# Element-strided squares and wider final stores in a fused attention and feed-forward kernel

## The chip, the cores and the metric

The kernel runs on one core of a Trainium2 chip. The metric is the device time of one execution in microseconds (us), the median over runs. Three runs of the kernel before gave 187.44, 187.94 and 187.97 us, so the median is 187.94 us.

A core has five engines that run side by side and wait for each other by semaphores. TensorE (PE in the profile; its weight loads are shown apart as PEld) multiplies matrices. ScalarE (ACT) and VectorE (DVE) compute elementwise. GpSimd (POOL) does small copies and memsets here. SyncE (SP) issues DMAs; ACT can issue DMAs too, on a hardware queue of its own.

## The reference, cut to what matters

```
phi(x)  = outer product of (S1 x) and (S2 x)          # 8 x 8 = 64 features per token
num     = phi(q) (phi(k)^T v),  den = phi(q) sum(phi(k)) + 1e-6
x       = num / den, heads side by side               # 4352 tokens x 128
h       = max(x @ w_in, 0)                            # 4352 x 2048
out     = (h * h) @ w_out                             # 4352 x 128, float32
```

The batch has 4 sequences of 1088 tokens. The part that matters here is the last line: each hidden value is rectified, squared, and multiplied by `w_out`.

## The kernel before, in words

Attention fills `xT`, which holds x transposed: 128 features on the partitions, 4352 token columns. Column 32·i + t of a sequence (t below 32, i below G = 34) is token 34·t + i, so 32 neighbouring columns are tokens that stand 34 apart in DRAM.

The feed-forward part walks over these columns in ten chunks (`FC`, line 135). Most are 448 or 512 columns wide; the first and the last are 256. The hidden width 2048 is cut into NB = 16 blocks of 128. A **unit** (line 560) is a chunk with as many blocks as fit into 512 result columns. The last chunk has 8 units of two blocks, called u0 to u7 here. A unit goes through four steps:

1. `ffn1` (L582): two matmuls, `w_in` block times the chunk's columns, into a PSUM tile `pg`. There are two such tiles in turn, so a unit's `ffn1` waits until the `relu` two units earlier has emptied its tile.
2. `relu` (L591), always on ACT: `pg` to the SBUF tile `gt`.
3. `square` (L599 on ACT or L601 on DVE): `gt` to the SBUF tile `g2`, which the profile names `g`. Its 512 columns are written in order.
4. `ffn2` (L615 in the last chunk, L620 in the others): accumulates over all 16 blocks. In the last chunk `g2` is the stationary operand, so that the result `po` comes out with tokens on the partitions: two token tiles of 128, the first in `po`, the second in `pol`.

A planner, `_Order.run` (lines 25 to 101), fixes the order of the instructions on each engine from estimated costs and due times. It decides which squares go to ACT and which to DVE. TensorE's own order is written out (lines 1043 to 1052): the two blocks of unit u in `ffn2` alternate with the two blocks of unit u + 4 in `ffn1` (LU = 4). For the last two units, all their blocks of the first token tile come before those of the second (line 1044), so the first tile is complete some 0.9 us earlier.

`f_last` (L642) then ends the kernel. ACT copies the first tile from PSUM to `obl` (L658), and `store(0)` sends it out; DVE copies the second tile (L660), and `store(1)` sends that. Column 32·x + t of a tile is on partition 32·x + t, so `store` (L648) issues four DMAs of 32 partitions, each going to 32 tokens that stand 34 rows apart: two on the SP queue and two on the ACT queue. A row is 128 floats, 512 bytes. The program ends when SP has seen the last DMA land (L1079).

Of the kernel before, what the change touches and what calls it, by code (L numbers as in the profile page):

```python
# [14 lines left out]
def _ap(t: bass.AP, p0: int, np_: int, off: int, free):  # L15
    p = list(t.ap)[0]
    return bass.AP(
        t.tensor, t.offset + p0 * p[0] + off, [[p[0], np_]] + [list(d) for d in free]
    )
# [85 lines left out]
def kernel(  # L105
# [11 lines left out]
    nc = tc.nc  # L117

    B, H, S, D = 4, 4, 1088, 32
    G = S // 32  # L120
# [20 lines left out]
    mult = mybir.AluOpType.mult  # L141
# [4 lines left out]
    Square = mybir.ActivationFunctionType.Square  # L146
# [111 lines left out]
    for i in range(2):  # L258
# [6 lines left out]
        out=own_f[:, :], in_=_ap(iden, 0, 128, 0, [[8, 16], [1, 8]]), op=add, axis=AX  # L265
# [13 lines left out]
    def banks(t_, x, col, n, k=2):  # L279

        return _ap(t_, 0, 128, 512 * x + col, [[512, k], [1, n]])
# [278 lines left out]
    units, first_unit, dur = [], {}, []  # L560
# [13 lines left out]
    last = len(FC) - 1  # L574
# [19 lines left out]
    def square(u, eng):  # L594
        w = units[u][2] * units[u][4]
        g2 = fpool.tile([128, 512], F32, tag="g2", bufs=G2, name="g2")
        gt = st["gt", u]
        if eng == "ACT":
            nc.scalar.activation(g2[:, 0:w], gt[:, 0:w], Square)  # L599
        else:  # L600
            nc.vector.tensor_tensor(out=g2[:, 0:w], in0=gt[:, 0:w], in1=gt[:, 0:w], op=mult)  # L601
        g2s[u] = g2

    def ffn2(u, i, xs=None):
# [37 lines left out]
    def f_last(c0):  # L642
        po, b = st["po", c0], B - 1


        def store(i):
            for x, eng in enumerate((nc.sync, nc.scalar, nc.sync, nc.scalar)):
                eng.dma_start(  # L648
                    bass.AP(
                        out.tensor,  # L650
                        out.offset + (b * S + (c0 - b * S) // 32 + 4 * i + x) * 128,
                        [[G * 128, 32], [1, 128]],
                    ),
                    ob[i][32 * x : 32 * x + 32, :],
                )

        ob = [fpool.tile([128, 128], F32, tag="obl", bufs=2, name="obl") for _ in range(2)]
        nc.scalar.copy(ob[0][:, :], po[0][:, 0:128])  # L658
        store(0)
        nc.vector.tensor_copy(ob[1][:, :], po[1][:, 0:128])  # L660
        store(1)
# [73 lines left out]
    for t0, n in ((0, 2), (2, 2), (4, 3), (7, 2)):  # L735
# [6 lines left out]
        out=_ap(qp0, 0, 128, 0, [[256, 2], [1, 256]]), in0=banks(x0, 2, 0, 256),  # L742
        in1=_ap(qb0, 0, 128, 0, [[256, 2], [1, 256]]), op=mult,
# [12 lines left out]
    def a_bd(x):  # L756
# [12 lines left out]
        out=_ap(zm, 0, 128, 0, [[16, 2], [8, 2], [1, 8]]),  # L769
        in0=_ap(st[0, "kvp"], 0, 128, 32, [[64, 2], [0, 2], [1, 8]]),  # L770
        in1=_ap(own_f, 0, 128, 0, [[0, 2], [8, 2], [1, 8]]),
        op=mult,
# [16 lines left out]
    for h in range(H):  # L789
# [19 lines left out]
        out=xT[:, 0:256], in0=num0[:, 0:256], in1=bc0[:, :], op=mult  # L809
# [184 lines left out]
    for u in range(NU):  # L994
        ci, c0, n, d0, m = units[u]
        w = n * m
# [7 lines left out]
        for i in range(m):  # L1004
# [12 lines left out]
            {"ACT": 0.095 + w / 1200, "DVE": dve(w)},  # L1017
            tu[u] - (0.6 if u > 1 else 40.0), [],
            lambda eng, u=u: square(u, eng), uses=[("relu", u)], rings=[("g2", G2)],
            late={"DVE": 0.0, "ACT": 0.2 if u > 1 else 0.0},  # L1020
        )
# [62 lines left out]
```

## Time and profile before

| what | value |
|---|---|
| timed runs | 187.44, 187.94, 187.97 us |
| span of the profiled execution, first to last instruction | 185.6 us |
| median of the runs less that span (start and end around the instructions) | 2.3 us |
| TensorE matmul busy | 180.1 us, 97% of the span |
| ScalarE busy | 147.4 us, 79% |
| VectorE busy | 109.4 us, 59% |
| GpSimd busy | 35.5 us, 19% |
| granted TensorE clock, mean | 0.998 |
| square on ACT, 128x512 (L599) | 79 of them, 629 ns each |
| square on DVE, 128x512 (L601) | 16 of them, 689 ns each |
| rectify on ACT, 128x512 (L591) | 95 of them, 587 ns each |

The profile's span runs from the first to the last instruction; the timed runs include what lies around it. No device time of its own is given for the profiled execution, so a change in the span is set against the median of the runs. Busy shares are averages over the whole span: what decides here happens in its last 15 us.

### The profile page before, as it was taken

The page shows a single profiled execution, that of the slowest core. Times are in us where ns is not written, and L with a number is a line of the kernel's source. Part 1 is how long each engine was busy: PE and PEld are TensorE (multiplying, and loading weights), DVE is VectorE, ACT ScalarE, POOL GpSimd, SP SyncE. Part 2 cuts the span into 40 slices and gives each one's busy share as a digit, 9 for nine tenths or more (in the row PEclk, how much of TensorE's full clock was granted, in tenths as well). Part 3 has the DMA queues.
Part 4 walks back from the last instruction along what each step waited for, and adds up shares of the span by engine and source line. Part 5 has one row for each costly group of instructions (what it writes and reads, how often), then busy time and mean ns, then how long its engine had stood idle before and what let it go on. Part 6 is the DMA issues. An engine that isn't in the chain of part 4 may idle for free.

```text
span 185.6 us, 3865 instructions
## 1 busy us (share of the span) xinstructions
PE 180.1 (97%) x1466; PEld 104.9 (57%) x1466; DVE 109.4 (59%) x244; ACT 147.4 (79%) x282; POOL 35.5 (19%) x157
## 2 busy tenths in 40 slices
PE   8898999999999999999999999999999999999992
PEld 2766766666656556554454545554555555555791
DVE  4979889958991699599343982996121113112210
ACT  3509778878978989699797996897999999988960
POOL 2725405327400000770000003820000000000000
PEclk9999999999999999999999999999999999999999
DMA  5799900100039600000882100001203000300111
GB/s 176 188 285 322 203 8 5 28 4 0 4 43 250 159 4 0 4 0 8 189 218 42 16 0 4 0 0 22 38 0 58 0 0 5 56 0 0 28 28 28
DMA packets 24673, 11.25 MB, mean 61 GB/s; under 512 B 18000, under 2 KB 23120, under 8 KB 24656
## 3 DMA queue, kind: packets, MB, share of 16 engines
q1 hardware_dynamic: 24144, 10.82, 24.8%
q10 hardware_dynamic: 512, 0.20, 0.4%
q8 instruction: 11, 0.18, 0.4%
q14 instruction: 6, 0.05, 0.1%
HBM read 8.78 MB, written 2.23 MB: 59 GB/s over the span
## 4 chain that ended last, share of the span: by engine, by line
PE 95%; DMA 1%; DVE 1%; ACT 0%; issue 0%; POOL 0%; ACTq 0%; DVEq 0%
PE po L620 60%; PE pg L582 18%; PE nd L535 3%; PE kvp L401 2%; PE pol L615 2%; PE po L615 2%; PE qc L303 2%; DMA s_nat<-in_S_dram 1%; PE kvp L383 1%; PE kf L313 1%; PE kc L303 1%; PE x L722 1%; ACT gt L591 0%; PE warm L671 0%; PE num L783 0%; PE den L783 0%
## 5 line engine op out<-in xcount | busy, mean ns | idle before, releaser
L620 PE MATMUL po<-g,w_o 128*128 128x512 f32 (+3 forms) x288 | 133.2, 546 | 0.0
L582 PE MATMUL pg<-xT,w_in 128*128 128x512 f32 (+3 forms) x160 | 104.5, 663 | 0.5 <-ACT gt L591 0.5
L591 ACT ACTIVATE gt<-pg 128x512 f32<-128x512 f32 (+3 forms) x145 | 80.9, 562 | 21.2 <-PE pg L582 20.5
L599 ACT ACTIVATE g<-gt 128x512 f32<-128x512 f32 (+2 forms) x123 | 72.0, 602 | 2.6
L620 PEld LDWEIGHTS po<-g,w_o 128*128 128x128 f32 x288 | 53.0, 189 | 29.8 <-issue 19.9
L582 PEld LDWEIGHTS pg<-xT,w_in 128*128 128x128 f32 x160 | 30.0, 189 | 31.7 <-issue 15.0
L601 DVE TENSOR_TENSOR g<-gt 128x512 f32<-128x512 f32 (+2 forms) x22 | 14.2, 651 | 41.8 <-ACT gt L591 41.8
L442 POOL COPY kv<-kvt 32x64 f32<-32x64 f32 x48 | 11.6, 241 | 64.7 <-DVE kvt L419 62.6
L496 POOL COPY rd<-rc 32x9 f32<-32x9 f32 (+2 forms) x80 | 16.6, 207 | 12.5 <-DVE rc L488 9.3
L505 DVE STREAM_SHUFFLE qa<-qc 128x576 f32<-128x576 f32 (+2 forms) x20 | 11.6, 647 | 0.0
L520 DVE TENSOR_TENSOR qp<-qa,qb 128x576 f32<-128x576 f32 (+2 forms) x20 | 10.8, 599 | 0.0
L624 DVE STREAM_TRANSPOSE oT<-po 128x512 f32<-128x512 f32 (+3 forms) x9 | 5.9, 652 | 8.1 <-PE po L620 8.1
L468 DVE STREAM_TRANSPOSE qt<-qc 128x576 f32<-128x576 f32 (+2 forms) x10 | 5.8, 614 | 6.0 <-PE qc L303 6.0
L354 DVE TENSOR_TENSOR kp<-fs 128x576 f32<-128x576 f32 x12 | 8.2, 741 | 0.0
L535 PE MATMUL nd<-qp,kv 32*32 32x288 f32 (+2 forms) x320 | 6.8, 353 | 0.0
L552 DVE TENSOR_TENSOR xT<-nd,bc 128x576 fp32r<-128x576 f32 (+2 forms) x10 | 5.6, 600 | 1.1 <-PE nd L535 1.1
L545 DVE STREAM_TRANSPOSE bc<-rd 128x576 f32<-128x576 f32 (+2 forms) x10 | 5.8, 598 | 0.7 <-POOL rd L496 0.6
L345 DVE STREAM_TRANSPOSE fs<-kc 128x576 f32<-128x576 f32 x6 | 4.3, 762 | 3.1 <-PE kc L303 3.1
L535 PEld LDWEIGHTS nd<-qp,kv 32*32 32x32 f32 x320 | 3.8, 103 | 4.0 <-issue 2.2
L505 DVE STREAM_SHUFFLE qb<-qc 128x576 f32<-128x576 f32 (+2 forms) x10 | 6.0, 648 | 0.0
L296 DVE STREAM_TRANSPOSE qT<-qn 128x192 f32<-128x192 f32 (+3 forms) x11 | 5.8, 562 | 0.0
L615 PE MATMUL pol<-w_o,g 128*128 128x128 f32 x32 | 5.7, 275 | 0.0
(94 smaller groups left out, 94.2 us busy)
## 6 DMA issues: line engine op xcount, KB each, us to landing
kn<-in_k_dram SPq DMA_DIRECT2D x3, 544.0 KB, 5.3
qn<-in_q_dram SPq DMA_DIRECT2D x3, 544.0 KB, 6.6
vn<-in_v_dram SPq DMA_DIRECT2D x9, 144.0 KB, 5.2
w_in<-in_moe_w_in_dram SPq DMA_DIRECT2D x4, 256.0 KB, 5.0
w_o<-in_moe_w_out_dram SPq DMA_DIRECT2D x4, 256.0 KB, 7.7
out_dram<-oT SPq DMA_DIRECT2D x12, 64.0 KB, 2.0
out_dram<-oT SPq DMA_DIRECT2D x8, 56.0 KB, 1.9
out_dram<-oT SPq DMA_DIRECT2D x8, 48.0 KB, 1.8
```

Source lines behind the costliest of these rows:

```text
L354: nc.vector.tensor_tensor(out=_ap(st[b, "kp"], 0, 128, 2 * o, [[64, NT], [8, 8], [1, 8]]), in0=_ap(fs, 0, 128, o, [[32, NT], [1, 8], [0, 8]]),
L442: nc.gpsimd.tensor_copy(_ap(st[b, "kv"], 32 * c, 32, 64 * h, [[32, E], [1, 32]]), _ap(st["kvt"], 32 * h, 32, 0, [[64, E], [1, 32]]),)
L496: nc.gpsimd.tensor_copy(st[b, "rd", i0][32 * h : 32 * h + 32, n * c : n * c + n], st["rc"][32 * c : 32 * c + 32, n * h : n * h + n],)
L505: nc.vector.stream_shuffle(in_=banks(st[b, "qc", i0], 2 * x, 0, m), out=_ap(st[b, which, i0], 0, 128, 2 * m * x, [[m, 2], [1, m]]), mask=m ...
L520: nc.vector.tensor_tensor(out=st[b, "qp", i0, e][:, r], in0=st[b, f"qa{e}", i0][:, r], in1=st[b, "qb", i0][:, r], op=mult,)
L535: nc.tensor.matmul(nd[32 * h : 32 * h + 32, 512 * c : 512 * c + m], kv[r, o : o + 32], qp[r, m * h : m * h + m], start=(e == 0), stop=(e = ...
L582: nc.tensor.matmul(st["pg", u][:, n * i : n * i + n], w_in[:, 128 * (d0 + i) : 128 * (d0 + i) + 128], xT[:, c0 : c0 + n],)
L591: nc.scalar.activation(gt[:, 0:w], st["pg", u][:, 0:w], Relu)
L599: nc.scalar.activation(g2[:, 0:w], gt[:, 0:w], Square)
L601: nc.vector.tensor_tensor(out=g2[:, 0:w], in0=gt[:, 0:w], in1=gt[:, 0:w], op=mult)
L615: nc.tensor.matmul(po[x // 128][:, 0:128], g[:, x : x + 128], w, start=(d == 0), stop=(d == NB - 1),)
L620: nc.tensor.matmul(po[0][:, 0:n], w, g, start=(d == 0), stop=(d == NB - 1))
```

## The change

Two places are edited, and they belong together.

In `square`, for units of the last chunk only, the 512 columns of `gt` are read in order, but the result is written with a stride. Within each group of 128 columns (one token tile), input column 32·j + t goes to output column 4·t + j. In the order of writing, 32 consecutive elements therefore land 4 floats (16 bytes) apart. The instruction has the same number of elements and the same engine as before.

This moves token 34·t + i to a partition that stands beside token 34·t + i + 1, so four neighbouring partitions hold four neighbouring rows of DRAM. In `f_last`, `store` therefore issues two DMAs of 64 partitions instead of four of 32: one on SP and one on ACT. Each covers 16 groups of four rows.

```diff
         gt = st["gt", u]
+        g_in, g_out = gt[:, 0:w], g2[:, 0:w]
+        if units[u][0] == last:
+            g_in = _ap(gt, 0, 128, 0, [[128, w // 128], [32, 4], [1, 32]])
+            g_out = _ap(g2, 0, 128, 0, [[128, w // 128], [1, 4], [4, 32]])
         if eng == "ACT":
-            nc.scalar.activation(g2[:, 0:w], gt[:, 0:w], Square)
+            nc.scalar.activation(g_out, g_in, Square)
         else:
-            nc.vector.tensor_tensor(out=g2[:, 0:w], in0=gt[:, 0:w], in1=gt[:, 0:w], op=mult)
+            nc.vector.tensor_tensor(out=g_out, in0=g_in, in1=g_in, op=mult)
...
         def store(i):
-            for x, eng in enumerate((nc.sync, nc.scalar, nc.sync, nc.scalar)):
+            for x, eng in enumerate((nc.sync, nc.scalar)):
                 eng.dma_start(
                     bass.AP(
                         out.tensor,
-                        out.offset + (b * S + (c0 - b * S) // 32 + 4 * i + x) * 128,
-                        [[G * 128, 32], [1, 128]],
+                        out.offset + (b * S + 16 * G * x + (c0 - b * S) // 32 + 4 * i) * 128,
+                        [[G * 128, 16], [128, 4], [1, 128]],
                     ),
-                    ob[i][32 * x : 32 * x + 32, :],
+                    ob[i][64 * x : 64 * x + 64, :],
                 )
```

The planner's costs are not edited. On every engine the instructions stand in the same order as before, with the same squares on ACT (six of the last chunk: u1 to u4, u6, u7) and on DVE (two: u0 and u5). Only the eight squares' shapes and the stores differ.

## The prediction

> **What bounds the kernel now.** I read the page first: the span, the busy shares, the chain that ended last.
>
> ```profile
> span 185.6 us, 3865 instructions
> ...
> PE 180.1 (97%) x1466; PEld 104.9 (57%) x1466; DVE 109.4 (59%) x244; ACT 147.4 (79%) x282; POOL 35.5 (19%) x157
> ...
> PE 95%; DMA 1%; DVE 1%; ACT 0%; issue 0%; POOL 0%; ACTq 0%; DVEq 0%
> ```
>
> TensorE is the bound up to its last matmul, and ACT carries nothing of the chain. So an edit of squares costs only what it makes TensorE wait, and an edit of stores counts only behind the last matmul. Both are read in the timeline of the last 15 us. First ACT in the last chunk (start, length, instruction, idle before it):
>
> ```profile
> 174.01 0.58 ACT L591 ACTIVATE gt<-pg 128x512 f32<-128x512 f32 x1
> 174.63 0.63 ACT L599 ACTIVATE g<-gt 128x512 f32<-128x512 f32 x1
> 175.16 0.58 ACT L591 ACTIVATE gt<-pg 128x512 f32<-128x512 f32 x1
> 175.78 0.63 ACT L599 ACTIVATE g<-gt 128x512 f32<-128x512 f32 x1
> 176.31 0.58 ACT L591 ACTIVATE gt<-pg 128x512 f32<-128x512 f32 x1
> 177.27 0.60 ACT L591 ACTIVATE gt<-pg 128x512 f32<-128x512 f32 x1 [0.38 <-PE pg L582]
> 177.90 0.63 ACT L599 ACTIVATE g<-gt 128x512 f32<-128x512 f32 x1
> 178.44 0.58 ACT L591 ACTIVATE gt<-pg 128x512 f32<-128x512 f32 x1
> 179.04 0.63 ACT L599 ACTIVATE g<-gt 128x512 f32<-128x512 f32 x1
> ```
>
> These are the rectify and square of u3, u4, the rectify of u5 (its square is on DVE), and both of u6 and u7. ACT works back to back: a pair takes 1.15 us (174.01 to 175.16), with a single gap of 0.38 us before u6. TensorE needs 1.12 to 1.13 us for a unit (175.15 to 176.28 below). ACT keeps up and no more; it is a second bound in this stage, though the page shows it at 79%. Next, the weight loads on TensorE that wait for ACT:
>
> ```profile
> 175.15 0.19 PEld L582 LDWEIGHTS pg<-xT,w_in 128*128 128x128 f32 x1
> ...
> 176.28 0.19 PEld L582 LDWEIGHTS pg<-xT,w_in 128*128 128x128 f32 x1
> ...
> 177.40 0.19 PEld L582 LDWEIGHTS pg<-xT,w_in 128*128 128x128 f32 x1
> ...
> 179.87 0.97 PEld L615 LDWEIGHTS po<-w_o,g 128*128 128x128 f32 x8
> ```
>
> The first three open `ffn1` of u5, u6 and u7. Each needs the `pg` tile that the rectify of u3, u4 or u5 empties at 174.59, 175.74 and 176.89. The last row holds four loads that read the square of u6 and four that read u7's; eight take 0.89 us up to the next group at 180.76, so the fifth starts near 180.31. u7's square ends at 179.67.
>
> **The slack.** The waits before these loads have 175.15 − 174.59 = 0.56, 0.54 and 0.51 us to spare, and u7's square has 180.31 − 179.67 = 0.64. From each I take 0.06 for the hand-over, an allowance of mine (ACT starts on a finished `pg` about 0.05 after its modelled end): 0.50, 0.48, 0.45, 0.58.
>
> **The strided squares.** Each of six ACT squares becomes longer by an unknown e, and each DVE square by about the same. The delays add up on ACT, which has no gap before u6. The rectify of u3 comes two squares late (2e), that of u4 3e, that of u5 4e. After that the gap of 0.38 is used up, and u7's square ends 6e − 0.40 late (0.38 and 0.02 of rounding). TensorE's delay is the largest of 2e − 0.50, 3e − 0.48, 4e − 0.45 and 6e − 0.40 − 0.58 = 6e − 0.98, or nothing. It begins at e = 0.45/4 = 0.11 us; above e = 0.27 the last term leads. The DVE squares don't lead: u0's ends 172.09 for a load at 173.57, u5's at 177.61 for one at 178.98, and at the e taken below u5's is 5e = 1.97 late against 1.37, so 0.66 with the hand-over, below 1.38.
>
> Behind a delayed TensorE stand only the rest of the last chunk's matmuls, both PSUM copies and the stores, so the delay goes to the end one for one.
>
> **What is e?** No row of ACT or DVE shows writes that hop at every element. From below: runs of 32 floats with hops between cost nothing on ACT (L432, 128x256, 377 ns, against 380 for L591 of that size), so the shape as such is free and e could be 0. The nearest row with a hop at every element is a memset on GpSimd, L710, which writes 36 floats 36 bytes apart. The rows of POOL's memsets:
>
> ```profile
> L246 POOL MEMSET sq<- x1: 313/313/313, 0.7 to 0.7; 128x256 f32 x1
> ...
> L248 POOL MEMSET vn<- x1: 125/125/125, 1.5 to 1.5; 128x32 f32 x1
> ...
> L710 POOL MEMSET pd<- x1: 156/156/156, 8.5 to 8.5; 128x36 f32 x1
> ```
>
> In order, an element costs (313 − 125)/224 = 0.84 ns, so 36 would take 125 + 4·0.84 = 128 ns. The hopping memset took 156, that is 28/36 = 0.77 ns more per element, nearly twice the price. For 512 elements e = 0.394 us. Another engine and rough spans: I keep e = 0 as the low end and twice this, 0.79 us, as the high end, and take 0.394, since it is the only row with the same kind of write.
>
> So TensorE is late by 6·0.394 − 0.98 = **1.38 us**. At e = 0 it is 0; at 0.79 it is 3.76.
>
> [...]
>
> **The stores.** The issues and landings behind the last matmul:
>
> ```profile
> 182.28 0.81 SPq L648 DMA_DIRECT2D out_dram<-obl  x2
> 182.31 0.85 ACTq L648 DMA_DIRECT2D out_dram<-obl  x2
> ```
> ```profile
> out_dram<-oT SPq DMA_DIRECT2D x12, 64.0 KB, 2.0
> ...
> out_dram<-oT SPq DMA_DIRECT2D x4, 32.0 KB, 1.7
> ...
> out_dram<-obl ACTq DMA_DIRECT2D x4, 16.0 KB, 1.6
> ```
>
> ACT's second issue takes 0.436 us of its 0.85, so it starts at 182.72, and its 16 KB lands 1.6 later at 184.32; SP's wait for that landing is 1.3 us long. One issue per queue starts at 182.31 and carries 32 KB. By the row of that size it lands in 1.7, at 184.01: **0.31 us earlier**. The bounds: 1.6 as for 16 KB gives 0.41; 2.0 as for 64 KB gives 0.00. The first tile's store also loses an issue per queue, which is worth nothing, since both queues then wait for the DVE copy that ends at 182.26. Nothing else is queued behind these issues.
>
> **Sum:** +1.38 − 0.31 = +1.07 us on a span of 185.6. The median 187.94 lies 2.3 above that span; that part is untouched, so 187.94 + 1.07 = **189.0 us**, 0.57% slower. About 0.3% (0.56 us) is what a measurement of this kernel can tell from no change. From e = 0.79 with no gain on the store: 187.94 + 3.76 = 191.7; with 0.31, 191.4. From e = 0 with the best store: 187.94 − 0.41 = 187.5.
>
> **Rivals.**
> - *The strided write is absorbed (not slower).* Mechanism: ACT writes hopping floats at its usual pace or nearly so, and the slack of 0.45 us at u5's rectify takes what remains. For it: reading and writing in runs is free in all rows, and ACT's clock need not be bound by its writes. Against: the hopping memset. It decides below e = (0.45 + 0.31)/4 = 0.19, where the delay equals the store's gain. At e = 0: 187.94 − 0.31 = 187.6 us.
> - *The hop costs far more, and ACT becomes the bound.* At e = 0.6 to 0.79 the delay is 2.62 to 3.76, minus 0.31: 190.3 to 191.4 us. For it: there is hardly any gap on ACT to absorb it. Against: the only row gives half that.
> - *The wider DMA gains nothing*, because 64 rows per DMA land like the 64 KB stores. With e = 0.394: 187.94 + 1.38 = 189.3 us. For it: landing grows with size in the rows above. Against: the 32 KB row.
>
> **How the numbers follow.** With the store at 0.31, the kernel is slower by more than 0.56 us from 6e − 0.98 − 0.31 = 0.56, so from e = 0.31. Forecast (e from 0.31 to 0.55, the store gaining): 0.45; its own range is 6·0.31 − 1.29 = 0.57 to 6·0.55 − 1.29 = 2.01 us, so 188.5 to 190.0. The wider DMA gaining nothing, with the same e: 0.06. Steep hop, e above 0.55: 0.18. Absorbed wholly or in part, e below 0.31: 0.31, of which e from 0.19 to 0.31 ends between no change and +0.56 and a smaller e between 187.5 and no change; I leave 0.05 of it for a saving above 0.56 us, if more than the issue went at the end. Slower by over 0.3%: 0.45 + 0.06 + 0.18 = 0.69, of which I move 0.03 to "within" because the forecast's lower edge lies on the bound: 0.66. Faster by over 0.3%: 0.05. Within: 0.26 + 0.03 = 0.29. The range takes in e = 0 with the best store and e = 0.79: 187.5 to 191.4; some 0.12 is left out.
>
> **What would show it.** In the profile after: ACT's six squares of the form 128x512 in the last chunk near 1.02 us and DVE's two near 1.1 instead of 0.63 and 0.69; ACT without its gap; TensorE idle before L582 of u5 to u7 with ACT as the releaser, and before the loads of u7; the L648 issues at one per queue and tile, landing in about 1.7 us. Squares still at 0.63 us would make the forecast wrong by its largest term; landings of 2.0 us or more would take the store's gain away.

## The result, and the profile after

The changed kernel takes 189.23 us, the kernel before 187.94 (medians of six runs each). The ratio is 1.0077, 95% interval 1.0065 to 1.0090, so the change costs 1.2 to 1.7 us. The ratio leaves out executions in a disturbed state, one of the changed kernel's six (192.63 us; the median of its other five is 189.11), and two of the traces below, of the kernel with x ordered beforehand and of the one with two strided squares, began their last chunk some 4 us late, so that of their times in it only distances are read.

The page after: first the span and the busy times, then the chain that ended last, by engine. Line numbers behind L597 are five higher than before.

```profile
span 187.0 us, 3860 instructions
...
PE 181.3 (97%) x1465; PEld 105.3 (56%) x1466; DVE 110.1 (59%) x244; ACT 150.0 (80%) x282; POOL 35.8 (19%) x157
...
PE 89%; ACT 5%; DMA 2%; issue 1%; DVE 1%; POOL 0%; ACTq 0%; DVEq 0%
```

ACT had 0% of the chain and now has 5%. Its busy time rose by 2.6 us (147.4 to 150.0). The timeline of ACT in the last chunk (start, length, instruction, idle before it):

```profile
171.90 0.60 ACT L591 ACTIVATE gt<-pg 128x512 f32<-128x512 f32 x1 [0.33 <-PE pg L582]
172.53 1.12 ACT L604 ACTIVATE g<-gt 128x512 f32<-128x512 f32 x1
173.46 0.63 ACT L591 ACTIVATE gt<-pg 128x512 f32<-128x512 f32 x1
174.12 1.15 ACT L604 ACTIVATE g<-gt 128x512 f32<-128x512 f32 x1
...
178.24 1.12 ACT L591 ACTIVATE gt<-pg 128x512 f32<-128x512 f32 x2
179.40 1.13 ACT L604 ACTIVATE g<-gt 128x512 f32<-128x512 f32 x1
180.32 0.63 ACT L591 ACTIVATE gt<-pg 128x512 f32<-128x512 f32 x1
180.99 1.14 ACT L604 ACTIVATE g<-gt 128x512 f32<-128x512 f32 x1
```

and the two squares on DVE:

```profile
171.61 1.10 DVE L606 TENSOR_TENSOR g<-gt 128x512 f32<-128x512 f32 x1 [3.68 <-ACT gt L591]
...
178.91 1.12 DVE L606 TENSOR_TENSOR g<-gt 128x512 f32<-128x512 f32 x1 [4.34 <-ACT gt L591]
```

The strided squares on ACT take 1.12 to 1.15 us instead of 0.63, the gap before u6 is gone (its rectify follows u5's, merged as x2), and a pair takes 174.12 − 172.53 = 1.59 us instead of 1.15. So the cadence (from one square's start to the next one's) grew by 0.44 to 0.45 (0.445 is used below), though a square grew by 0.51: the next rectify, itself 0.05 us longer, starts 0.19 us before a long square ends (172.53 + 1.12 = 173.65 against 173.46), and only 0.10 before a short one ended. The weight loads on TensorE that now wait, with the releaser in brackets:

```profile
175.74 0.19 PEld L582 LDWEIGHTS pg<-xT,w_in 128*128 128x128 f32 x1 [0.30 <-ACT gt L591]
...
177.33 0.19 PEld L582 LDWEIGHTS pg<-xT,w_in 128*128 128x128 f32 x1 [0.39 <-ACT gt L591]
...
178.93 0.19 PEld L582 LDWEIGHTS pg<-xT,w_in 128*128 128x128 f32 x1 [0.38 <-ACT gt L591]
...
182.17 0.52 PEld L620 LDWEIGHTS po<-w_o,g 128*128 128x128 f32 x4 [0.26 <-ACT g L604]
```

These are the four places that the prediction named: `ffn1` of u5, u6 and u7 wait for the rectify, and the fifth of the last group of loads waits for u7's square. The brackets count idle time only, 1.33 us together. By their starts, set against the cadence of the same loads before, the four come 0.39, 0.47, 0.47 and 0.33 us late, 1.66 together, which is TensorE's whole delay in the table below. The stores, from the timeline of the SP and ACT queues and from the list of landings (KB each, us from issue to landing):

```profile
183.22 1.47 SPq L653 DMA_DIRECT2D out_dram<-obl  x2
183.22 1.56 ACTq L653 DMA_DIRECT2D out_dram<-obl  x2
...
183.82 0.29 DVE L665 COPY obl<-pol 128x128 f32<-128x128 f32 x1 [3.79 <-PE pol L620]
```
```profile
out_dram<-obl SPq DMA_DIRECT2D x2, 32.0 KB, 1.9
out_dram<-obl ACTq DMA_DIRECT2D x2, 32.0 KB, 2.1
```

There is one issue per queue and tile, as intended, but it lands (its semaphore takes its last step) 1.9 to 2.1 us after the issue, where the smaller one took 1.5 to 1.6.

Where the span's 1.41 us (187.04 − 185.63) come from, by the two traces:

| part | before | after | difference |
|---|---|---|---|
| start of the span to u1's rectify | 171.70 | 171.90 | +0.20 |
| u1's rectify to the copy of the second tile (TensorE's end) | 10.27 | 11.91 | +1.65 |
| that copy's end (182.26, 184.11) to the last landing (184.35, 186.20) | 2.09 | 2.09 | 0.00 |
| last landing to the end of the span | 1.28 | 0.84 | −0.44 |

The first row is no effect of the change: ACT's copy at L432 already starts at 12.96 us instead of 12.71, 160 us ahead of the first edited instruction. Without it the trace shows +1.21 us.

### The profile page after: what moved, and what is told of

Same layout as the page of the kernel before. It is cut to its first block, busy times and chain, and to the rows that moved or that the text cites. A ratio compares the mean times of both kernels' runs of the same rounds, so it can differ in the third digit from the quotient of the medians.

```text
span 187.0 us, 3860 instructions
## 1 busy us (share of the span) xinstructions
PE 181.3 (97%) x1465; PEld 105.3 (56%) x1466; DVE 110.1 (59%) x244; ACT 150.0 (80%) x282; POOL 35.8 (19%) x157
## 4 chain that ended last, share of the span: by engine, by line
PE 89%; ACT 5%; DMA 2%; issue 1%; DVE 1%; POOL 0%; ACTq 0%; DVEq 0%
PE po L625 58%; PE pg L582 17%; PE nd L535 3%; ACT g L604 3%; ACT gt L591 2%; PE kvp L401 2%; DMA s_nat<-in_S_dram 2%; PE qc L303 2%; PE kvp L383 1%; PE kf L313 1%; PE kc L303 1%; PE x L727 1%; PE pol L620 0%; PE po L620 0%; PE num L788 0%
## 5 line engine op out<-in xcount | busy, mean ns | idle before, releaser
L625 PE MATMUL po<-g,w_o 128*128 128x512 f32 (+3 forms) x288 | 133.2, 546 | 0.0
L604 ACT ACTIVATE g<-gt 128x512 f32<-128x512 f32 (+2 forms) x123 | 75.1, 627 | 2.6
L625 PEld LDWEIGHTS po<-g,w_o 128*128 128x128 f32 x288 | 53.0, 189 | 29.8 <-issue 19.9
L606 DVE TENSOR_TENSOR g<-gt 128x512 f32<-128x512 f32 (+2 forms) x22 | 15.1, 690 | 43.6 <-ACT gt L591 43.5
L620 PE MATMUL po<-w_o,g 128*128 128x128 f32 x32 | 5.9, 277 | 0.1
```

Of the source, the lines that this page charges most:

```text
L604: nc.scalar.activation(g_out, g_in, Square)
L606: nc.vector.tensor_tensor(out=g_out, in0=g_in, in1=g_in, op=mult)
L620: nc.tensor.matmul(po[x // 128][:, 0:128], g[:, x : x + 128], w, start=(d == 0), stop=(d == NB - 1),)
L625: nc.tensor.matmul(po[0][:, 0:n], w, g, start=(d == 0), stop=(d == NB - 1))
```

## The experiments

**Squares alone, first try.** The changed kernel with four stores per tile, cut to its own order of rows:

```diff
-            for x, eng in enumerate((nc.sync, nc.scalar)):
+            for x, eng in enumerate((nc.sync, nc.scalar, nc.sync, nc.scalar)):
...
-                        out.offset + (b * S + 16 * G * x + (c0 - b * S) // 32 + 4 * i) * 128,
-                        [[G * 128, 16], [128, 4], [1, 128]],
+                        out.offset + (b * S + 8 * G * x + (c0 - b * S) // 32 + 4 * i) * 128,
+                        [[G * 128, 8], [128, 4], [1, 128]],
...
-                    ob[i][64 * x : 64 * x + 64, :],
+                    ob[i][32 * x : 32 * x + 32, :],
```

> The strided squares as in the changed kernel, with four stores per token tile as before (each of 32 partitions, now 8 groups of four rows). First theory, the squares cost all of it: ACT's six squares near 1.14 us, u7's load about 1.65 us late, and the time 187.9 + 1.65 = 189.6 us, or 0.0 to 0.5 us above the changed kernel, which lost four issues. Rival, the wide stores themselves cost time (their issues took 0.55 to 0.66 us in the changed kernel's trace against 0.33 to 0.44 before, and landed 1.8 to 2.2 us after the issue against 1.4 to 1.6): this kernel is then 0.3 us or more faster than the changed one, below 188.9 us.

Measured: 190.55 us, ratio to before 1.0169 (1.0154 to 1.0183), slower than either theory said. TensorE is late by what the theory gives (u1's rectify to the last copy 11.91 us), but the last store lands 3.66 us after the copy ends (187.53 against 183.87) instead of 2.09. Of the 1.57 more, 1.09 is the later start of the last issue (1.56 after the copy instead of 0.47), the rest its longer way to landing:

```profile
L653 SPq DMA_DIRECT2D out_dram<-obl x4: 661/664/819, 183.0 to 185.3; - x4
L653 ACTq DMA_DIRECT2D out_dram<-obl x4: 734/744/790, 183.0 to 185.4; - x4
```

The columns are shortest, median and longest issue in ns. A store of 8 groups of four rows is issued in 0.66 to 0.82 us, about twice the 0.33 to 0.44 of 32 rows at one distance, and its semaphore rises in 9 steps where the other's rises in 16. What makes it slower is not shown. The run changed two things at once and decides nothing on the wide stores.

**Squares alone, stores untouched.** The first hunk of the change only.

> The strided squares alone, the stores exactly as in the kernel before (so the rows of the last chunk go to wrong tokens). The first try at this gave its stores a new shape, whose issues took 0.67 to 0.82 us and whose last landing came 1.6 us later, so it didn't isolate the squares. Theory: TensorE ends 1.65 us late against the start of the last chunk, and nothing else changes: 1.65 us slower than before on the same chip, ratio 1.0088. Rival, what the changed kernel lost was partly its stores: ratio below 1.0070.

Measured: 189.25 us against 187.47, ratio 1.0091 (1.0078 to 1.0105), so 1.5 to 2.0 us. In its trace u1's rectify to the last copy is 11.91 us, the last landing 2.10 us after the copy (186.01 − 183.91) and the end 1.28 later, both as before. The squares cost 1.65 us, and the stores lost nothing in the changed kernel.

**Stores alone.** The second hunk of the change only.

> The squares in order as before, the stores as in the changed kernel; the rows of the last chunk go to wrong tokens, so the output differs from the reference there. First theory: all squares at 0.63 and 0.69 us, TensorE without a wait in the last chunk; the last store lands as long after the last copy as before (about 2.1 us), and what the end of the program may save is at most 0.45 us: 187.5 to 187.9 us. Rival, the wide stores cost time: 188.2 us or more.

Measured: 187.08 us against 187.42, ratio 0.9982 (0.9972 to 0.9993): 0.1 to 0.5 us faster. The trace has 10.26 us from u1's rectify to the last copy, 2.10 from the copy to the last landing (184.297 − 182.194), and 0.84 from there to the end. The wide stores gain only behind the last landing. The two hunks add up: 1.0091 times 0.9982 is 1.0073, beside the measured 1.0077.

**Where the end gains.** Before the program ends, SP checks the DMAs' eight completion semaphores, which are used in turn (a ring), and two of the copies': five checks of a pair each, in a fixed order. From the traces (us; the check that the last landing releases in brackets):

```
kernel        last landing   SP's checks start at
before        184.35         [184.37] 184.44 184.51 184.58 184.64
after         186.20          184.73  184.80 185.41 186.00 [186.22]
```

Before, the store that lands last has the semaphore checked first, and four more checks of some 0.067 us follow, 0.27 in all. After, it has the one checked last: with four final DMAs instead of eight, the last of them stands elsewhere in the ring of eight semaphores. To separate this from the number of stores, the ring is moved in the kernel before, by four:

```diff
-        load_k(nc.sync, b)
+        if b == B - 1:
+            for c in range(0, S, 256):
+                load_k(nc.sync, b, c, min(c + 256, S))
+        else:
+            load_k(nc.sync, b)
```

> The kernel before; only the load of the last sequence's k, some 80 us before the end, is cut into five DMAs instead of one, which moves the final stores on by four in the ring of eight completion semaphores. The store that lands last then has the semaphore that SP checks last instead of first. Theory, part of what wide stores save is the place of that semaphore: SP's checks after the last landing fall from five to one, 0.27 us less between the last landing and the end of the span (1.28 us before), ratio about 0.9986. Rival, the end is shorter because fewer DMAs were issued: no change, ratio 1.000.

Measured: 187.13 us against 187.47, ratio 0.9981 (0.9971 to 0.9991). The trace has 1.02 us from the last landing (184.83) to the end (185.85), 0.26 less than before, with the four old stores and 2.07 us from copy to landing. So 0.26 of the 0.44 us is the semaphore's place, and this alone is worth as much in the timing as the wide stores, whose interval it shares. The other 0.17 us stands behind ACT's last DRAIN instruction: it starts some 0.3 us late and takes some 135 ns in the kernel before, in this one and in the next one, which has two stores on ACT instead of four, and takes 8 ns without delay in the changed kernel. What makes it late was not found.

**Is it rows or DMAs that the stores pay for?** The kernel before with two stores per tile and 64 neighbouring rows per DMA:

```diff
-            for x, eng in enumerate((nc.sync, nc.scalar, nc.sync, nc.scalar)):
+            for x, eng in enumerate((nc.sync, nc.scalar)):
...
-                        out.offset + (b * S + (c0 - b * S) // 32 + 4 * i + x) * 128,
-                        [[G * 128, 32], [1, 128]],
+                        out.offset + (c0 + 128 * i + 64 * x) * 128,
+                        [[128, 64], [1, 128]],
...
-                    ob[i][32 * x : 32 * x + 32, :],
+                    ob[i][64 * x : 64 * x + 64, :],
```

> Squares in order; each token tile is stored by two DMAs of 64 partitions as in the changed kernel, but to 64 rows that follow each other in DRAM (one level of rows instead of 16 groups of four; the rows go to other tokens than they belong to, and overwrite some). Theory, the pattern of rows makes the wide stores slow to issue and to land: issues back to 0.33 to 0.44 us, the last landing about 0.3 us sooner after the last copy than 2.1, and the time 0.3 us below the 187.1 of the kernel with only the wide stores. Rival, 64 rows per DMA make it: issues of 0.55 to 0.66 and 187.1 us.

Measured: 187.48 us against 187.83, ratio 0.9987 (0.9973 to 1.0001). The issues:

```profile
L648 SPq DMA_DIRECT2D out_dram<-obl x2: 471/512/553, 181.4 to 182.3; - x2
L648 ACTq DMA_DIRECT2D out_dram<-obl x2: 535/550/565, 181.4 to 182.3; - x2
```

They take 0.47 to 0.57 us: 0.08 to 0.1 less than with groups of four rows, but 0.13 more than with 32 rows, and the last landing comes 2.08 us after the copy, as before within 0.02. Neither expectation holds as put: doubling the rows does most of it, grouping them by four the rest. The traces' packets say the same. From the start of ACT's last issue to its first packet it takes 0.94 us with 32 rows (182.73 to 183.67), 1.48 with 64 in groups of four (184.14 to 185.62) and 1.39 with 64 neighbouring ones (182.35 to 183.74). One issue instead of two starts the last DMA 0.44 us sooner after the copy (0.03 instead of 0.47), and the first packet of its 64 rows then comes 0.45 to 0.54 us later after the issue. That is where the expected gain went. In these stores rows, partitions and bytes double together, so which of them counts is not shown. For the issue, bytes are the smaller part: SP's stores of `oT` in the kernel before, all from 32 partitions, take 0.32 us for the first of a group, with 16 KB and with 64 KB alike, and behind another mostly 0.43 (16 KB) and 0.49 to 0.51 (64 KB). For the time to the first packet no run here separates them.

**Do the delays on ACT add up, or does each square have its price?** The changed kernel with the stride on two squares far apart, u1 and u7, and then on four in a row, u1 to u4 (`NU - 7 <= u <= NU - 4` in the same line):

```diff
-        if units[u][0] == last:
+        if u in (NU - 7, NU - 1):
```

> The changed kernel with the stride on two of the eight squares only, u1 and u7 (the rows of the last chunk are then partly mixed up, so the output differs). Theory, ACT's delays add up until slack runs out: a strided square holds ACT 0.45 us longer; u1's delay is taken by the gap before u6 and lies below the slack of every wait (0.45 and more), and u7's square, 0.51 us longer, still ends before its load (slack 0.58): TensorE is not delayed, and from u1's rectify start to TensorE's end it takes 10.27 us as before. Rival, each strided square costs its own share, 1.65/6 = 0.28 us: 10.8 us.

> The changed kernel with the stride on u1 to u4 only (all on ACT; the output differs as in the run before). Theory: the rectify of u5 comes 4 times 0.445 = 1.78 us late against a slack of 0.45, so TensorE is 1.33 us late, 11.6 us from u1's rectify start to TensorE's end. Rival, an equal share per square: 4 times 0.28 = 1.10 us, 11.37 us.

Measured from u1's rectify to the last copy: 10.26 us with two (175.56 to 185.82), 11.58 with four (172.47 to 184.05). Two strided squares cost nothing and four cost 1.31 us, so a price per square is excluded. With two, no load waits for ACT; with four, the same three as in the changed kernel do, and none waits for a square:

```profile
176.31 0.19 PEld L582 LDWEIGHTS pg<-xT,w_in 128*128 128x128 f32 x1 [0.30 <-ACT gt L591]
...
177.90 0.19 PEld L582 LDWEIGHTS pg<-xT,w_in 128*128 128x128 f32 x1 [0.38 <-ACT gt L591]
...
179.49 0.19 PEld L582 LDWEIGHTS pg<-xT,w_in 128*128 128x128 f32 x1 [0.38 <-ACT gt L591]
```

**What makes a strided square slow.** Two middle chunks with their squares in ten forms, one chunk on ACT and one on DVE:

```diff
+        if ci in (6, 7):
+            eng = "DVE" if ci == 7 else "ACT"
...
+                2: ([[128, 4], [1, 128]], [[1, 4], [4, 128]]),
...
+                5: ([[256, 2], [2, 128], [1, 2]], [[2, 2], [4, 128], [1, 2]]),
...
+            gi, go = _ap(gt, 0, 128, 0, P[0]), _ap(g2, 0, 128, 0, P[1])
```

> Only the lengths of instructions are read from this run; its output is not the reference's, since the squares of two middle chunks are written in other orders (one chunk's squares all on ACT, the next one's all on DVE). Ten forms of the 128x512 square: in order; writes that hop by 2, 4, 8 or 32 floats at each element; writes in pairs of adjacent floats that hop by 4; reads that hop by 2, 4 or 32 at each element; reads in such pairs. First theory, an element that does not stand beside its neighbour costs a second access: hopping writes near 1.14 us on ACT and 1.10 on DVE whatever the step, pairs at 0.63 and 0.69, hopping reads like writes. Rival, only steps of a 16-byte line or more cost: a step of 2 stays at 0.63 and 0.69. Second rival, only writes cost: hopping reads stay at 0.63 and 0.69.

The groups by line (L616 to L625 are the ten forms on ACT, L626 to L635 on DVE; count, busy us and mean ns):

```profile
L619 ACT ACTIVATE g<-gt 128x512 f32<-128x512 f32 x2 | 2.3, 1146 | 0.0
...
L620 ACT ACTIVATE g<-gt 128x512 f32<-128x512 f32 x2 | 2.3, 1131 | 0.0
L618 ACT ACTIVATE g<-gt 128x512 f32<-128x512 f32 x2 | 2.3, 1128 | 0.0
...
L628 DVE TENSOR_TENSOR g<-gt 128x512 f32<-128x512 f32 x2 | 2.2, 1092 | 0.4 <-ACT gt L591 0.4
...
L626 DVE TENSOR_TENSOR g<-gt 128x512 f32<-128x512 f32 x2 | 1.4, 692 | 9.5 <-ACT gt L591 9.5
L627 DVE TENSOR_TENSOR g<-gt 128x512 f32<-128x512 f32 x2 | 1.4, 689 | 0.4 <-ACT gt L591 0.4
L621 ACT ACTIVATE g<-gt 128x512 f32<-128x512 f32 x2 | 1.4, 680 | 0.0
L617 ACT ACTIVATE g<-gt 128x512 f32<-128x512 f32 x2 | 1.3, 674 | 0.1
...
L616 ACT ACTIVATE g<-gt 128x512 f32<-128x512 f32 x2 | 1.3, 631 | 0.1
L623 ACT ACTIVATE g<-gt 128x512 f32<-128x512 f32 x1 | 1.2, 1237 | 0.0
...
L634 DVE TENSOR_TENSOR g<-gt 128x512 f32<-128x512 f32 x1 | 1.2, 1199 | 0.0
...
L624 ACT ACTIVATE g<-gt 128x512 f32<-128x512 f32 x1 | 1.1, 1077 | 0.0
```

In ns, ACT then DVE (the forms up to the written pairs ran twice on each engine, the reading ones once):

| form | written so | read so |
|---|---|---|
| in order | 631, 692 | 631, 692 |
| hop of 2 floats (8 bytes) | 674, 689 | 672, 691 |
| hop of 4 (16 bytes) | 1128, 1092 | 1237, 1095 |
| hop of 8 | 1146, 1092 | not tried |
| hop of 32 | 1131, 1080 | 1077, 1199 |
| pairs, hop of 4 | 680, 698 | 671, 703 |

The first theory falls at the hop of 2: those elements don't stand beside their neighbours and cost no more than pairs do (674 and 689 ns against 680 and 698). The second rival falls too, since reads pay like writes. What paid in the table is a hop of 16 bytes or more at each element: with 16, written, (1128 − 631)/512 = 0.97 ns more on ACT and (1092 − 692)/512 = 0.78 on DVE. A longer hop adds nothing to writes (1146 and 1131 ns on ACT, 1092 and 1080 on DVE); single reads with a hop of 32 took 0.16 us less than with 4 on ACT and 0.10 more on DVE, the dearest hop there with (1199 − 692)/512 = 0.99 ns. A hop of 3 floats was not tried, so where between 8 and 16 bytes the price begins is not shown, nor what causes it.

**The order made where it is free.** Squares in order, wide stores; x is put in the new order once, on GpSimd:

```diff
+        if b == B - 1 and x == 1:
+            nc.gpsimd.tensor_copy(
+                _ap(xl, 0, 128, 0, [[128, 2], [1, 4], [4, 32]]),
+                _ap(xT, 0, 128, FC[last][0], [[128, 2], [32, 4], [1, 32]]),
+            )
...
-            xT[:, c0 : c0 + n],
+            xl[:, 0:n] if ci == last else xT[:, c0 : c0 + n],
```

> The same order of tokens and the same wide stores as the changed kernel, but the order is made once: GpSimd copies the last chunk's 256 columns of x in the new order as soon as they are there, long before the chunk begins; all squares are written in order. First theory: the squares are the whole loss and one hopping write off the path is free: as the kernel with only the stores changed, 187.5 to 187.9 us. Rival, the order of tokens or the wide stores cost something by themselves: 188.2 us or more.

Measured: 187.21 us against 187.42, ratio 0.9975 (0.9964 to 0.9987). The trace shows the one hopping write:

```profile
L560 POOL CAST xl<-xT x1: 693/693/693, 132.9 to 132.9; 128x256 fp32r<-128x256 f32 x1
```

The write starts at 132.9 us, 40 us before the chunk begins, and the distance from u1's rectify to the last copy is 10.26 us. The kernel's rows stand in the same order as the changed kernel's. It is 0.2 to 0.7 us faster than the kernel before, and by the two ratios some 1.9 us faster than the changed one. Its gain is that of the wide stores and their semaphores, within the intervals.

**The order made by TensorE's reads.** Squares in order, wide stores; `ffn1` of the last chunk reads x with hops:

```diff
-            xT[:, c0 : c0 + n],
+            _ap(xT, 0, 128, c0, [[128, n // 128], [1, 32], [32, 4]])
+            if ci == last else xT[:, c0 : c0 + n],
```

> Same order of tokens and same wide stores as the changed kernel, squares written in order; the order is made by TensorE, which reads the last chunk's columns of x (the moving operand of its 16 first matmuls) 32 floats apart. Theory, an operand read with a hop at every element is slowed on TensorE as it was on ACT and DVE: the 16 matmuls of 256 columns take longer than their 0.36 to 0.40 us and stand on the path, since TensorE is the bound: at 1.7 times their cadence (0.11 us between starts of the loads around them) up to 16 x 0.09 = 1.4 us, 188.6 us against 187.4 before. Rival, TensorE reads with a hop at no cost: 187.1 us, as the kernel that orders x on GpSimd.

Measured: 187.44 us against 187.83, ratio 0.9991 (0.9978 to 1.0004). From u1's rectify to the last copy it takes 10.46 us, 0.19 more than in order. The theory is off by a factor of seven; the median matmul of these has 378 ns instead of 364, and 16 times 14 ns is 0.22 us. Hopping reads cost TensorE something here, but little.

## Why the prediction was right

The forecast of 189.0 us lies 0.2 below the measured 189.23, and its +1.07 us a little below the 1.2 to 1.7 that the ratio gives. The mechanism of the larger term, the squares, held in every part that was tried; that of the smaller one, the stores, did not. By the traces the squares' term was 0.27 us too small (1.38 for 1.65) and the gain at the end 0.13 too small (0.31 for 0.44), so that one miss made up for half of the other.

- **ACT as a second bound.** Right. TensorE waited at the places named, and the addition of delays predicted nothing for two strided squares and 1.33 us for four; measured were 0.00 and 1.31. (These two numbers use the 0.445 read after the change; the rule that adds the delays is the prediction's.)
- **e, the size of one square's delay.** Too small: 0.394 from GpSimd's memset against 0.51 in the length of a square and 0.445 in ACT's cadence. With 0.445 the prediction's own sum, 6e − 0.98, gives 1.69 us; the trace has 1.65, the timing of the squares alone 1.5 to 2.0. The forecast had 1.38. The overlap of neighbours on ACT, which grows with a long square (0.19 us for 0.10), was not thought of; had the length been guessed right without it, the sum would have been 6·0.51 − 0.98 = 2.08, too much.
- **Why an element costs more.** Right for this hop, wrong as a rule: the row chosen was read as a price of every hop. The probe shows that a hop of 8 bytes is free within 0.05 us (674 and 689 ns against 631 and 692), and the memset's elements are 36 bytes apart, so that it stood on the paying side was luck of that row.
- **The rise on DVE.** As said: 1.10 to 1.12 us, never the last to arrive.
- **The stores.** The step that failed is "by the row of that size it lands in 1.7". That row's stores have 32 partitions, with 8 runs of 128 bytes each, and are issued by SP alone. Here ACT's 64 rows land 2.1 us after the issue, and 2.09 after the copy, as before: the term is 0.00 instead of 0.31. The rival in which the wider DMA gains nothing had this right.
- **What stood in its place.** 0.44 us behind the last landing, 0.26 of it from the place of one semaphore in SP's checks. The prediction saw that SP waits for the landing, and not that four more checks follow it. That the gain at the end came out near the forecast, −0.44 for −0.31, is chance.

The page was no help with this: ACT's share rose from 79% to 80%, and the price lay in a stage of 12 us where ACT had a single gap of 0.38.

## What to carry to other kernels

Put an access that hops by 16 bytes at each element where it runs once and early, here 256 columns of x on an idle engine (0.69 us at 132.9, and still 10.26 us from u1's rectify to the last copy), and not into the repeated step of an engine that just keeps pace (1.65 us lost). Before lengthening an instruction, read the gaps of its engine in that stage of the timeline and add the delays up to each wait of the bound engine: what fitted into the slack cost nothing here (0.00 us with two strided squares), and the rest nearly in full (1.31 of 1.33 us with four). When stores at the end are merged, count what each DMA then carries and what follows the last landing, not only the DMAs: here 0.00 us was gained up to the landing and 0.44 behind it.

## What the runs showed of the hardware

- A square of 512 fp32 columns that hops by 16 bytes at each element took about 0.97 ns more per element on ACT and 0.78 on DVE when written so, and reads with hops of 16 and 128 bytes cost too (0.87 to 1.18 on ACT, 0.79 to 0.99 on DVE, one sample each); hops of 8 bytes and pairs were free within 0.05 us for 512 elements, and written hops of 32 and 128 bytes cost no more than 16 (within 0.02 us).
- TensorE reading its moving operand 128 bytes apart lost 14 ns on a matmul of 256 columns (median 378 ns instead of 364).
- Issue and start of a final store grew with its rows (and bytes, 512 a row): 0.33 to 0.44 us for 32 rows, 0.47 to 0.57 for 64, 0.55 to 0.66 for 64 in groups of four; the first packet came 0.94, 1.39 and 1.48 us after the start of ACT's last issue.
- With four final stores per tile of 8 groups of four rows, the last landing came 1.6 us later after the last copy than with four of 32 rows at one distance (3.66 us instead of 2.09); 1.09 of it was the start of the last issue.
- The place of the last store's semaphore in the final checks was worth 0.26 us of span, and moving it by cutting one load 80 us earlier made the kernel before 0.1 to 0.3% faster.
